# Position-bias features moved off GpSimd in an attention + soft-MoE kernel, with a new step order

## The chip, the core and the metric

One core of a Trainium2 chip runs the whole program. Its engines are PE (TensorE), DVE (VectorE), ACT (ScalarE), POOL (GpSimd) and SP (SyncE, which here only issues transfers). The metric is the device time of one execution in microseconds, as the median of three runs.

## What is computed

Attention with a position bias that a small network makes from relative positions, and behind it a soft mixture of experts over all 4608 tokens. All data are float32.

```python
# q, k, v: (8, 8, 576, 64); w1: (1, 32), b1: (32,), w2: (32, 8)
scores = q @ k.T / 8
x = log1p(|i - j|) / log1p(max(i, 1))              # one number per pair of positions
bias = relu(x[..., None] @ w1 + b1) @ w2           # 32 features, then 8 heads
attn = softmax(scores + bias) @ v                  # -> x: (4608, 512)
# phi: (512, 32); 8 experts, 4 slots each; w1: (8, 512, 1024), w2: (8, 1024, 512)
logits = x @ phi
slots  = softmax(logits, over tokens).T @ x        # 32 slots
slot_out[e] = relu(slots[e] @ w1[e]) @ w2[e]
out = softmax(logits, over slots) @ slot_out
```

## The kernel before

The program is a list of small steps. A string `ORDER` names every step once, and the steps' instructions are emitted in that order; each engine then runs its own instructions in the order in which they were emitted, and waits only for data and for buffers. A token such as `S1/5+@0,2` is step `S1` of unit 5, with the PSUM banks 0 and 2, and the `+` switches the step to its other form (another engine, or for `S` another way to cut the product). So `ORDER` alone decides queues, banks, and which engine takes a copy.

**Bias stage.** The bias depends on the position only through a table, so 36 jobs (`bias_job`) build it. A job i has four feature steps `f{i}.0` to `f{i}.3` (lines 925 to 934): each takes the table `tabs`, 304 to 576 wide by the job, times a scale, and clips it below. DVE and POOL do this with one `tensor_scalar` (line 933); ACT with a Relu (line 931). `B{i}` multiplies the four with the second layer (PE, line 944), `E{i}` copies the product out of PSUM with its constant (ACT line 957, DVE line 955), and `D{i}` writes it to DRAM (line 966). `b{c}` reads back the bias of a row stripe c of 128 query rows (line 390), once its eight jobs are written.

**Attention.** 40 units are (head pair, batch) pieces: 16 short ones for the first head pair, then 24 whole ones. In a unit `S{p}` makes the scores of 128 query rows for two heads, in 4 products of 128 rows (line 495) or, with `+`, in 8 of 64 rows (line 501); each product is two instructions. `t` adds the bias and finds the minimum (DVE, line 513), `e` is the exponential (ACT, line 521), `a` and `m` finish its sum (lines 528 and 532), `n` scales by it (POOL, line 398). `T` and `R` turn the result by 64-row pieces (`half_turn`, line 460), `c` and `cR` copy it out (ACT or DVE, line 401), `M0` to `M2` multiply with v (line 601), `x` copies, `xs` stores. `lq` and `lv` load q, k and v.

**Experts.** The units 32 to 39 also carry the tokens through the expert stage: `fx` fetches the stored heads (line 626), `K01`, `K23` and `KR` turn them, `L` makes logits (line 681), `lc` copies them, `D` sums them over heads, `d1` finds minima, `d2` is the exponential, `dq` keeps a copy of the logits, `W` and `C` turn, `Z` makes slot inputs. In units 38 and 39 `J` and `F` steps merge the two halves of the softmax. Then, all under unit 39: `F0` to `F7` are the experts' first layer (line 1029), `H` its Relu, `U0` and `U1` turn the hidden activations (line 1051), `V` copies them, `s{cg}.{Q}` is the second layer (line 1102), `so`, `g`, `ss` gather its result, `k` stacks the token weights, `o{cg}.{q}` and `X{cg}` make outputs (lines 1128 and 1142), `p` and `px` copy these out of PSUM, `P` (512 KB) and `PX` (256 KB) store them. `w`, `A` and `r` load the experts' 64 weight tiles of 512 KB (line 911). All of these transfers are issued by SP, in the order of `ORDER`.

## Time and profile before

| | |
|---|---|
| median of three runs | 574.61 us (574.53 to 574.68) |
| profiled execution | 575.72 us, of which span 573.9 us |
| busy in the span | PE 537.8, DVE 438.8, ACT 427.8, POOL 280.8 us |
| mean granted TensorE clock | 0.988 of full speed |

The span runs from the first to the last instruction. Each engine's busy time is the union of its instructions' times, so instructions that overlap count once. PE is busy in 94% of the span, and the idle part lies mostly in the first 80 us and behind 500 us. A "wait" line names who ended an engine's idle time; "issue" means that nothing in the profile explains the wait.

### The profile page before, as it was taken

What the parts mean: (1) busy time and instruction counts of PE and PEld (TensorE: products, weight loads), DVE (VectorE), ACT (ScalarE), POOL (GpSimd) and SP (SyncE); (2) the same over time, 40 slices, a digit from 0 to 9 for tenths busy, and PEclk for the clock granted to TensorE, in tenths of its full rate; (3) what the DMA queues carried; (4) which work ended last, traced back from release to release, by engine and by line L of the source; (5) the groups of instructions that cost most, each with busy time, mean ns of one, the idle gap of its engine ahead of it and who ended that gap; (6) DMA issues with size and microseconds to landing.
All of it is one profiled execution on the core that took longest, in us unless ns stands there. A gap on an engine that the chain in (4) does not pass through costs nothing.

```text
span 573.9 us, 23164 instructions
## 1 busy us (share of the span) xinstructions
PE 537.8 (94%) x9735; PEld 353.6 (62%) x9735; DVE 438.8 (76%) x1196; ACT 427.8 (75%) x935; POOL 280.8 (49%) x396
## 2 busy tenths in 40 slices
...
GB/s 136 269 198 208 204 175 326 286 295 278 250 118 138 136 55 126 183 245 89 158 189 167 81 100 211 162 270 154 269 98 122 105 61 284 326 334 366 334 333 327
DMA packets 46264, 117.12 MB, mean 204 GB/s; under 512 B 5457, under 2 KB 9681, under 8 KB 46161
## 3 DMA queue, kind: packets, MB, share of 16 engines
...
q10 hardware_dynamic: 144, 0.29, 0.2%
...
## 4 chain that ended last, share of the span: by engine, by line
PE 67%; DVE 11%; DMA 11%; ACT 4%; issue 3%; POOL 1%; DVEq 0%; SPq 0%; ACTq 0%
PE ps L601 19%; PE ps L460 15%; PE ps L501 14%; PE ps L495 5%; DVE mem L933 4%; DMA mem<-in_qk_dram 4%; DVE mem L513 4%; PE ps L944 3%; PE ps L1102 3%; PE ps L1029 2%; ACT mem L521 2%; DMA bias_m<-mem 2%; PE ps L681 2%; DMA xs<-mem 2%; DMA mem<-bias_m 1%
## 5 line engine op out<-in xcount | busy, mean ns | idle before, releaser
L398 POOL TENSOR_SCALAR mem<-mem,ms 128x576 f32<-128x576 f32 x288 | 212.4, 754 | 125.5 <-DVE ms L532 72.1
L513 DVE CUSTOM_DVE_ANT_0 mem<-ps,mem 128x576 f32<-128x576 f32 x288 | 207.9, 751 | 46.2 <-PE ps L501 31.9
L521 ACT ACTIVATE mem<-mem,ms 128x576 f32<-128x576 f32 x288 | 221.6, 774 | 24.8 <-DVE ms L513 21.4
L401 ACT COPY mem<-ps 128x1024 f32<-128x1024 f32 (+6 forms) x213 | 143.7, 698 | 53.9 <-PE ps L460 36.4
L601 PE MATMUL ps<-mem 64*64 64x288 f32 (+2 forms) x2880 | 161.8, 360 | 0.4
L401 DVE COPY mem<-ps 128x1024 f32<-128x1024 f32 (+6 forms) x143 | 114.4, 820 | 41.7 <-PE ps L1128 14.0
L501 PE MATMUL ps<-mem 64*64 64x64 f32 (+1 forms) x1648 | 125.0, 409 | 3.5 <-DVE ms L513 1.9
L460 PE MATMUL ps<-ident,mem 64*128 64x64 f32 x2976 | 119.8, 227 | 6.2 <-DMA mem<-xs 2.3
L460 PEld LDWEIGHTS ps<-ident,mem 64*128 64x128 f32 x2976 | 106.3, 140 | 25.8 <-issue 9.6
L601 PEld LDWEIGHTS ps<-mem 64*64 64x64 f32 x2880 | 98.8, 135 | 29.6 <-DVE ms L513 0.6
L501 PEld LDWEIGHTS ps<-mem 64*64 64x64 f32 x1648 | 68.1, 133 | 67.4 <-issue 46.5
L521 ACT ACTIVATION_READ_ACCUMULATOR mem<-mem,ms 128x1 f32 x288 | 55.9, 194 | 0.0
L495 PE MATMUL ps<-mem 64*128 64x512 f32 (+1 forms) x328 | 54.0, 435 | 1.5 <-DMA mem<-in_qk_dram 1.5
L933 POOL TENSOR_SCALAR mem<-mem,nb 128x336 f32<-128x336 f32 (+16 forms) x25 | 50.0, 2007 | 7.3 <-PE ps L944 4.0
L933 DVE TENSOR_SCALAR mem<-mem,nb 128x304 f32<-128x304 f32 (+17 forms) x81 | 49.2, 662 | 0.0
L528 POOL TENSOR_SCALAR ms<-ms 128x2 f32<-128x2 f32 x62 | 13.8, 223 | 71.3 <-ACT mem L521 68.4
L944 PE MATMUL ps<-mem,wbd 128*32 128x512 f32 (+41 forms) x480 | 38.4, 441 | 8.9 <-DVE mem L933 6.8
L495 PEld LDWEIGHTS ps<-mem 64*128 64x128 f32 x328 | 33.5, 187 | 20.0 <-issue 15.6
L944 PEld LDWEIGHTS ps<-mem,wbd 128*32 128x32 f32 x480 | 14.3, 109 | 28.0 <-issue 11.2
L957 ACT ACTIVATE mem<-ps,bcon 128x591 f32<-128x591 f32 (+20 forms) x35 | 19.7, 610 | 13.4 <-PE ps L944 13.3
L931 ACT ACTIVATE mem<-mem,cols 128x560 f32<-128x560 f32 (+15 forms) x38 | 27.2, 764 | 1.9 <-DVE mem L1204 1.7
L532 DVE RECIPROCAL ms<-ms 128x2 f32<-128x2 f32 x144 | 21.9, 160 | 6.7 <-POOL ms L528 5.1
...
## 6 DMA issues: line engine op xcount, KB each, us to landing
...
mem<-in_qk_dram SPq DMA_DIRECT2D x32, 576.0 KB, 4.6
...
mem<-bias_m SPq DMA_DIRECT2D x20, 576.0 KB, 5.4
...
```

The lines of the kernel that those rows point to most:

```text
L398: nc.gpsimd.tensor_scalar(out=out, in0=y, scalar1=r, scalar2=1.0, op0=ALU.mult, op1=ALU.mult)
L401: (nc.vector.tensor_copy if eng else nc.scalar.copy)(out=out, in_=in_)
L460: nc.tensor.matmul(out, src[rs], ident[rs, rs], is_transpose=True, start=True, stop=True, tile_position=(64 * r, 0))
L495: nc.tensor.matmul(pss[hh].t[:, n, 0:w], x[rs, S + QP[p]:S + QP[p] + P], x[rs, ks], start=True, stop=True, tile_position=(64 * hh, 0))
L501: nc.tensor.matmul(pss[hh].t[64 * r:64 * r + 64, n, 0:w], x[rs, q0:q0 + 64], x[rs, ks], start=True, stop=True, tile_position=(64 * hh, 64 ...
L513: nc.vector.tensor_tensor_reduce(out=d["y", p][:, :, hh], in0=blocks(d["ps", p][hh].read().rearrange("a n j -> a (n j)")[:, 0:S]), in1=blo ...
L521: nc.scalar.activation(out=y, in_=y, func=AF.Exp, bias=d["mn", p][:, hh:hh + 1], scale=-1.0, accum_out=d["sm", p][:, hh:hh + 1])
L532: nc.vector.reciprocal(out=r, in_=r)
L601: nc.tensor.matmul(d["po"].t[64 * c:64 * c + 64, hh, 0:n], d["v"][rs, 64 * k:64 * k + 64], turned(u)[rs, k, c, cs], start=k == 0, stop=k = ...
L931: nc.scalar.activation(out=f, in_=tabs[:, 0:n], func=AF.Relu, bias=cols[:, 1:2], scale=sc)
L933: (nc.gpsimd if eng else nc.vector).tensor_scalar(out=f, in0=tabs[:, 0:n], scalar1=sc, scalar2=nb1[:, 0:1], op0=ALU.mult, op1=ALU.max)
L944: nc.tensor.matmul(x[32 * t:32 * t + 32, o0 + c0:o0 + c1], wbd, f, start=True, stop=True, tile_position=(0, 32 * t))
```

## The change

Three edits in code, and a new `ORDER` for all 2649 steps.

- The features: a `+` on a feature step now always means ACT. Before, a `+` on the fourth feature of a job (`t = 3`) meant POOL. Of the 144 features DVE had 81, ACT 38 and POOL 25; now DVE has 94, ACT 50 and POOL none.
- `turn_hidden`: the 8 turns of 128x128 for each half become 16 turns of 64 rows, and `keep_hidden` reads the new layout. The copies keep their size.
- In the new order `dq` stands behind `d2` throughout ("logits' copy behind their exponentials").

```diff
         def feats(eng, t):
             f = fb[t] = room(FW * place_of["f"][f"f{i}.{t}"], n)
             sc = scl[:, scales[t]:scales[t] + 1]
-            relu[t] = eng and t < 3
-            if relu[t]:
+            relu[t] = eng
+            if eng:
                 nc.scalar.activation(out=f, in_=tabs[:, 0:n], func=AF.Relu, bias=cols[:, 1:2], scale=sc)
             else:
-                (nc.gpsimd if eng else nc.vector).tensor_scalar(out=f, in0=tabs[:, 0:n], scalar1=sc, scalar2=nb1[:, 0:1],
-                                                                op0=ALU.mult, op1=ALU.max)
+                nc.vector.tensor_scalar(out=f, in0=tabs[:, 0:n], scalar1=sc, scalar2=nb1[:, 0:1], op0=ALU.mult, op1=ALU.max)
...
     def turn_hidden(Q):
         h = ends["U", Q] = Banks(2, 2)
-        for z in range(2):
-            for x in range(4):
-                nc.tensor.transpose(out=h.t[:, z, x * P:(x + 1) * P], in_=ends["hS", Q][:, z, x * P:(x + 1) * P],
-                                    identity=ident)
+        for x in range(8):
+            for r in range(2):
+                half_turn(h.t[:, r, 64 * x:64 * x + 64], ends["hS", Q][:, x // 4, x % 4 * P:x % 4 * P + P], r)
...
-        cp(z, hT2[Q][:, 4 * z:4 * z + 4, :], ends["U", Q].read()[:, z].rearrange("a (x n) -> a x n", x=4))
+        cp(z, hT2[Q].rearrange("a x (r n) -> a r x n", r=2)[:, z], ends["U", Q].read()[:, z].rearrange("a (x n) -> a x n", x=8))
...
 ORDER = """
-f11.0/-1 f11.1/-1 f14.1/-1+ f14.2/-1+ f15.0/-1+ f11.2/-1 f14.3/-1 f11.3/-1+ f14.0/-1 wm/-1 f15.3/-1+ B11/-1@0
...
+f11.2/-1+ f13.1/-1 f13.3/-1+ f10.3/-1+ f13.2/-1 f13.0/-1 wm/-1 f10.2/-1+ f11.1/-1+ B13/-1@0 f11.0/-1+ f9.1/-1+ f9.0/-1+
...
```

The step marks also move in number: of the `S` steps 41 were cut in whole 128-row products and 30 are now; of the 36 `E` copies 25 were on ACT and 23 are now.

How the engines' queues change, at three places. First POOL at the start of the program. L933 is a feature, L528 the step `a`, L398 the step `n`, `nb_96` the clipping constant. Before:

```order
masks.py:199 AFFINE_SELECT ident<-ident 128x128
L933 TENSOR_SCALAR mem<-mem,nb_96 128x400
L933 TENSOR_SCALAR mem<-mem,nb_96 128x336
L933 TENSOR_SCALAR mem<-mem,nb_96 128x368
L933 TENSOR_SCALAR mem<-mem,nb_96 128x432
L933 TENSOR_SCALAR mem<-mem,nb_96 128x336
```

Now:

```order
masks.py:199 AFFINE_SELECT ident<-ident 128x128
L528 TENSOR_SCALAR ms<-ms 128x2 x2
L398 TENSOR_SCALAR mem<-mem,ms 128x9x64 x2
L528 TENSOR_SCALAR ms<-ms 128x2
L398 TENSOR_SCALAR mem<-mem,ms 128x9x64 x3
```

The features that opened POOL's queue are gone, and its first work is the scaling of the first exponentials.

Second PE at the last unit's expert stage, from the last product with v (L601) on. L460 is a 64-row turn (of `et`: `W`; of `lq`: `C`; of `mem`: `K01`, `K23`, `KR`), L862, L872 and L876 are `J` steps, L681 is `L`, L823 and L826 are `Z/38`, L696 and L698 are `D`, L882 is `F2` of the merge. Before:

```order
L601 MATMUL ps<-mem 64x288 x36
L862 MATMUL ps<-ident,stM_82 1x128 x2
L460 MATMUL ps<-ident,et_81 128x64 x3
L460 MATMUL ps<-ident,mem 128x64 x16
L460 MATMUL ps<-ident,lq 128x64 x3
L681 MATMUL ps<-mem,phis 32x288 x16
L872 MATMUL ps<-ident,et 128x1
L823 MATMUL ps<-mem,ek 32x512 x4
L826 MATMUL ps<-mem,ek 32x128 x4
L696 MATMUL ps<-lp,rsum 32x512
```

Now:

```order
L601 MATMUL ps<-mem 64x288 x36
L460 MATMUL ps<-ident,et_81 128x64 x3
L460 MATMUL ps<-ident,lq 128x64 x3
L862 MATMUL ps<-ident,stM_82 1x128 x2
L681 MATMUL ps<-mem,phis 32x288 x16
L872 MATMUL ps<-ident,et 128x1
L823 MATMUL ps<-mem,ek 32x512 x4
L826 MATMUL ps<-mem,ek 32x128 x4
L696 MATMUL ps<-lp,rsum 32x512
```

The turn `C` (of `lq`) moved ahead of the first step that reads the fetched heads, that first step is now `L` and no longer `K01`, and `K01` stands behind `D`.

Third SP at the end of the program: the weight loads, then the stores of 512 KB (L1136 before, L1134 now) and of 256 KB (L1151, now L1149). Before:

```order
L911 DMA mem<-in_moe_w_dram 128x1024 x28
L1136 DMA out_dram<-mem 128x1024 x8
L1151 DMA out_dram<-mem 128x512
L1136 DMA out_dram<-mem 128x1024 x4
L1151 DMA out_dram<-mem 128x512 x2
L1136 DMA out_dram<-mem 128x1024 x3
```

Now:

```order
L911 DMA mem<-in_moe_w_dram 128x1024 x28
L1134 DMA out_dram<-mem 128x1024 x3
L1149 DMA out_dram<-mem 128x512 x2
L1134 DMA out_dram<-mem 128x1024 x4
L1149 DMA out_dram<-mem 128x512
L1134 DMA out_dram<-mem 128x1024 x8
```

Three large stores now precede the first two small ones (`PX1`, `PX2`) where eight did. On PE the second layer's third column group (`s2`) and the small outputs `X0` to `X2` now stand directly behind `o0.0` and `o0.1`, ahead of `o1.0` and `o1.1`.

## Rows read from the trace of the kernel before

**Rows 1.** The page: busy time of each engine, its share of the span, and instructions.

```profile
PE 537.8 (94%) x9735; PEld 353.6 (62%) x9735; DVE 438.8 (76%) x1196; ACT 427.8 (75%) x935; POOL 280.8 (49%) x396
```

**Rows 2.** Busy time by stretch: PE, PEld, DVE, ACT, POOL, clock, DMA share, GB/s.

```profile
5.20:35.20 30.00, 22.65 (x302) 10.61 (x301) 29.86 (x55) 21.71 (x34) 29.68 (x16) 1.00 0.56 199
...
5.20:93.80 88.60, 76.80 (x1162) 43.66 (x1161) 85.50 (x196) 72.05 (x138) 70.25 (x59) 0.98 0.63 209
...
200.00:300.00 100.00, 99.20 (x1736) 67.08 (x1736) 80.39 (x224) 82.48 (x185) 54.29 (x85) 1.00 0.45 146
```

**Rows 3.** PE's waits between 5 and 94 us: total us, times, longest.

```profile
PE ps L944 <- DVE mem L933: 6.8, 7, 2.3
PE ps L944 <- DVE ms L513: 1.9, 3, 1.2
```

**Rows 4.** Features alone by stretch: DVE and POOL (L933), then ACT (L931).

```profile
5.20:93.80 88.60, 49.20 (x81) 49.23 (x25) 0.98 0.63 209
...
35.20:93.80 58.60, 20.18 (x32) 19.55 (x9) 0.97 0.66 214
...
5.20:93.80 88.60, 26.36 (x37) 0.98 0.63 209
```

**Rows 5.** Timeline of DVE and POOL: start, us, engine, line, count, idle before.

```profile
38.28 1.38 DVE L933 TENSOR_SCALAR mem<-mem,nb 128x496 f32<-128x496 f32 x3
...
38.98 6.95 POOL L933 TENSOR_SCALAR mem<-mem,nb 128x448 f32<-128x448 f32 x3 [4.02 <-PE ps L944]
...
49.01 4.50 POOL L398 TENSOR_SCALAR mem<-mem,ms 128x576 f32<-128x576 f32 x6
...
50.62 0.83 DVE L933 TENSOR_SCALAR mem<-mem,nb 128x448 f32<-128x448 f32 x1
```

**Rows 6.** The page's groups: score products by form, count, busy, mean ns, idle before.

```profile
L501 PE MATMUL ps<-mem 64*64 64x64 f32 (+1 forms) x1648 | 125.0, 409 | 3.5 <-DVE ms L513 1.9
...
L495 PE MATMUL ps<-mem 64*128 64x512 f32 (+1 forms) x328 | 54.0, 435 | 1.5 <-DMA mem<-in_qk_dram 1.5
```

**Rows 7.** Timeline of PE: the first two scores of unit 8, S0 and S3.

```profile
93.81 2.27 PE L501 MATMUL ps<-mem 64*64 64x512 f32 x32
```

**Rows 8.** Timeline of PE and ACT at the last expert stage; busy time by stretch.

```profile
505.38 1.12 PE L460 MATMUL ps<-ident,mem 64*128 64x64 f32 x16 [2.31 <-DMA mem<-xs]
...
506.26 0.42 PE L460 MATMUL ps<-ident,lq 64*128 64x64 f32 x3
...
512.51 0.63 ACT L401 COPY lp<-ps 64x576 f32<-64x576 f32 x1 [1.29 <-DVE mb L719]
...
505.38:517.83 12.45, 11.46 (x200) 6.88 (x200) 7.52 (x23) 5.28 (x12) 0.38 (x2) 0.86 0.79 293
```

**Rows 9.** Timeline of PE: turns by 64 rows, the hidden activations' turns, the second layer.

```profile
52.32 0.71 PE L460 MATMUL ps<-ident,mem 64*128 64x64 f32 x16 [0.33 <-DVE ms L513]
...
531.70 1.97 PE L1051 MATMUL ps<-ident,mem 128*128 128x128 f32 x16
...
542.45 0.41 PE L1102 MATMUL ps<-mem 128*32 128x128 f32 x4 [1.68 <-issue]
```

**Rows 10.** Timeline of the outputs: products, second layer, stores issued by SP.

```profile
544.32 2.06 PE L1128 MATMUL ps<-cT,ss 32*128 32x512 f32 x16
...
546.80 7.99 SPq L1136 DMA_DIRECT2D out_dram<-mem  x8
...
549.02 3.70 PE L1102 MATMUL ps<-mem 128*32 128x128 f32 x128
...
552.65 0.50 PE L1142 MATMUL ps<-small,ss 32*128 32x128 f32 x8
...
554.90 1.15 SPq L1151 DMA_DIRECT2D out_dram<-mem  x1
```

**Rows 11.** Busy time and DMA by stretch at the end, columns as in rows 2.

```profile
547.50:571.50 24.00, 15.35 (x338) 10.73 (x332) 8.67 (x12) 8.62 (x13) 0.00 (x0) 0.90 1.00 392
540.78:542.45 1.67, 0.00 (x0) 0.00 (x0) 0.00 (x0) 0.00 (x0) 0.00 (x0) 1.00 0.91 361
```

More of the change, by code (lines that the diff above doesn't have):

```diff
@@ new lines @@
+a3/34+ n2.1/34 t2.0/35#0 a4/34+ m4/34 m3/34 t2.1/35 n4.0/34 n3.1/34 W/32@0 KR/32@4 wc/32 T1/34@6 w20/39 w10/39 w21/39
+w22/39 w11/39 w8/39 w12/39 lq/36 lv/34 R1/34@0 x/33+ lv/35 fx/33 krc/32+ n3.0/34 T0/34@2 krd/32 c1/34 cR1/34+ T2/34@4
+c2/34 S3/35+@0,6 c0/34+ t3.0/35#1 t3.1/35 e2.0/35 S0/35@2,4 T3/34@0 Z/32@6 t0.1/35#2 t0.0/35 R3/34@2 n4.1/34 e2.1/35
+e3.0/35 c3/34 R4/34@0 cR3/34+ cR4/34 zc/32 L/33@4 e0.0/35 lc/33 C/32@0 T4/34@2 cA/32 K23/33@6 kc23/33 S1/35+@4,0
+c4/34+ t1.0/35#5 t1.1/35 S0/36+@2,6 e3.1/35 a3/35 e0.1/35 t0.1/36#4 t0.0/36 m3/35 e1.1/35 K01/33@4 KR/33@0 krc/33+
@@ new lines @@
+krd/33 D/33@6 e1.0/35 d1/33 n3.0/35 d2/33 a2/35 a0/35+ e0.0/36 m0/35 a1/35 m2/35 n2.1/35 n0.0/35 n3.1/35 n0.1/35
+dq/33+ n2.0/35 M0/34@2 M1/34 S1/36+@0,6 t1.1/36#3 t1.0/36 m1/35 n1.1/35 M2/34 x/34+ lq/37 fx/34 W/33@6 e0.1/36 kc01/33
+wc/33 R3/35@4 T3/35@0 cR3/35 T2/35@6 c2/35 n1.0/35 S2/36@2,4 c3/35+ d3/33 t2.1/36#1 a0/36+ e2.1/36 e1.1/36 R1/35@0
+Z/33@6 cR1/35+ t2.0/36 e2.0/36 zc/33 S4/36@0,4 t4.0/36#0 T1/35@2 K23/34@6 t4.1/36 e1.0/36 c1/35 kc23/34+ L/34@0
+KR/34@4 lc/34 krc/34 T0/35@2 C/33@0 a1/36+ m1/36 krd/34+ c0/35 K01/34@6 D/34@5 cA/33 S3/36+@0,2 d1/34 t3.0/36#5 m0/36
@@ new lines @@
+kc01/34 d2/34 dq/34+ e4.0/36 e4.1/36 M0/35@6 S2/37+@0,4 fx/35 lq/38 M1/35 M2/35 n0.0/36 n0.1/36 t3.1/36 a2/36+ a4/36
+m4/36 n4.0/36 n4.1/36 t2.1/37#2 m2/36 n2.1/36 e3.0/36 e3.1/36 W/34@2 R4/36@4 lv/36 lv/37 t2.0/37 n2.0/36 e2.0/37 wc/34
+cR4/36 x/35+ T4/36@0 a3/36+ c4/36+ m3/36 n1.0/36 n1.1/36 n3.1/36 n3.0/36 T2/36@2 c2/36 S0/37@6,4 T0/36@0 Z/34@2 c0/36
+t0.1/37#0 d3/34 t0.0/37 R3/36@0 zc/34 S3/37@6,4 e2.1/37 t3.1/37#1 R1/36@2 cR3/36 e0.1/37 cR1/36 K01/35@0 K23/35@2
+kc01/35 a2/37+ kc23/35 t3.0/37 T3/36@4 T1/36@6 c3/36 c1/36+ L/35@0 lc/35 KR/35@2 krc/35 e3.1/37 e0.0/37 S1/37@4,6
@@ new lines @@
+e2.0/38 t3.1/38 d1/36 M0/37@0 e3.1/38 cB/33 d2/36 dq/36 m1/38 cC/32 S4/38@6,4 M1/37 t4.0/38#0 S3/39+@2,6 t4.1/38
+e3.0/38 a3/38+ M2/37 cB/35 e4.0/38 d3/36 m3/38 a2/38 n1.1/38 n0.0/38 n0.1/38 n1.0/38 e4.1/38 t3.0/39#4 C/36@2 KR/36@4
+t3.1/39 m2/38 x/37 cA/36 krc/36+ W/36@6 K23/36@0 T1/38@2 krd/36 wc/36 kc23/36+ cB/36 a4/38 n2.1/38 n3.1/38 lv/38
+n2.0/38 S1/39@4,6 R1/38@0 n3.0/38 m4/38 n4.1/38 c1/38 Z/36@2 t1.1/39#3 t1.0/39 n4.0/38 e3.0/39 cB/34 cR1/38 R4/38@0
+R3/38@6 zc/36 T4/38@4 cR4/38 cR3/38 e3.1/39 c4/38+ T2/38@0 S0/39@2,6 c2/38 A6/39 A1/39 fx/37 A2/39 A9/39 e1.0/39
@@ new lines @@
+T0/38@4 a3/39 m3/39 c0/38 L/37@0 t0.1/39#2 t0.0/39 T3/38@6 K01/37@2 lc/37 S2/39@0,4 c3/38+ kc01/37 e0.1/39 e0.0/39
+e1.1/39 t2.1/39#5 t2.0/39 KR/37@6 K23/37@2 D/37@4 d1/37 d2/37 a1/39+ m1/39 n1.0/39 n3.1/39 a0/39+ m0/39 n1.1/39
+n0.0/39 n0.1/39 krd/37 kc23/37+ e2.1/39 cC/33 dq/37+ M0/38@0 M1/38 M2/38 W/37@2 e2.0/39 d3/37 krc/37+ wc/37 T1/39@4
+T0/39@6 a2/39 m2/39 n2.1/39 A3/39 lv/39 A10/39 fx/38 A8/39 x/38 cC/34 A7/39 A4/39 R1/39@2 cR1/39+ c1/39 c0/39 Z/37@0
+K01/38@2 n2.0/39 n3.0/39 R3/39@4 A11/39 A5/39 A12/39 cR3/39 zc/37 L/38@6 lc/38 T3/39@0 T2/39@4 kc01/38+ c2/39 c3/39+
```

324 lines of the change are left out of this document (150 added, 174 removed).

## The prediction, made before the changed kernel was run

> **What bounds the kernel now.** I read the page first: PE is busy in 94% of the span [rows 1], so most of the time is PE's own work, and only two things can move it: PE's idle time, and how much work the order gives it. Next I read the busy times by stretch. In the middle PE leaves 0.8 of 100 us idle [rows 2]; nothing is to be won there but cheaper instructions. Between 5.2 and 93.8 us it is busy for only 76.8 of 88.6 us, so 11.8 us go there. DVE is what bounds that stretch: it is busy for 85.5 of 88.6 us, and in the first 30 us for 29.86 of 30 [rows 2]. PE's waits confirm it: 6.8 us for features that DVE makes and 1.9 us for DVE's bias additions are its longest ones there [rows 3]. ACT has 16.5 us free in the same stretch (72.05 busy). I end the stretch where PE starts the scores of unit 8, since all features and all but none of the bias products are done then [rows 7].
>
> At the end another thing bounds. From 547.5 to 571.5 us the DMA engines are full (share 1.00, 392 GB/s) with the stores [rows 11]: 16 of 512 KB and 4 of 256 KB are 9.4 MB, which is 24 us at that rate. There PE's work counts only as far as it lets the first stores begin and keeps the queue fed.
>
> The sum below is made on the profiled execution: 575.72 us, 1.82 us of it outside the span, 1.11 us above the median of 574.61. I take the differences over to the median.
>
> **The front, 5.2 to 93.8 us.** Before, the 81 features on DVE take 49.20 us, 0.61 each, and POOL's 25 take 49.23 us, 1.97 each [rows 4]. Three wide ones that DVE ran one after the other, while POOL stood idle until 38.98 us for most of their time, took 1.38 us together, 0.46 each [rows 5]. The mean feature on DVE is a bit narrower (429 wide against 496), so I take 0.45. So 81 x (0.61 - 0.45) = 12.7 us of DVE's time is lengthening by POOL, if all of it is. It goes with POOL's features. DVE pays 13 more features, 13 x 0.45 = 5.9 us, and two bias copies E that ACT gives up, which I price as a feature on ACT, 26.36 / 37 = 0.71 [rows 4], so 1.4 us. Busy after: 85.5 - 12.7 + 5.9 + 1.4 = 80.1 us. ACT pays 12 more features at 0.71 and loses the two copies: 72.05 + 8.5 - 1.4 = 79.2 us. Neither POOL nor PE is near that (PE 76.8).
>
> So after the change two engines have 80 us of work where one had 85.5. How much they idle no row shows. DVE as the only bound idled 3.1 us; ACT, bound by DVE, 16.5. Two engines of equal load that feed each other idle more than one; I take 6 us, twice DVE's, since ACT's queue opens with 10 features in a row and has no product to wait for early. That ends the stretch at 86 instead of 88.6: **-2.6 us**. The bounds: 80.1 + 3.1 = 83.2, that is -5.4; and ACT idling as now, 79.2 + 16.5 = 95.7, that is +7.1. Behind the stretch PE has work without end, so the gain stays.
>
> The rows on POOL's slowing can be set beside the Trainium skill, SBUF, "Who interferes with whom": a DVE `tensor_scalar` in its two-port mode and a GpSimd instruction take a shared port pair in turn, each for its whole length, and the other stands still. The trace agrees that both are slow together (0.61 and 1.97 us); by this rule the scaling steps that stay on POOL would still slow DVE, which gives the first rival below.
>
> **Scores.** 41 steps with whole products take 54.0 us, 1.32 each, and the 103 cut ones 125.0 us, 1.21 each [rows 6]. Eleven steps change form: 11 x 0.1 = **-1.1 us**, on PE and so on the path. Bounds 0 (neighbours on PE overlap them) and -1.5.
>
> **The last expert stage.** PE stands 2.31 us until the heads of the last batch are fetched [rows 8]. The turn C (0.42 us) now stands ahead of that wait, so it costs nothing: -0.4. Then from 505.38 to the first layer at 517.83 us PE works 11.46 of 12.45 us [rows 8]. Now L comes first, so lc, D and d1 start earlier while K01, K23 and KR still fill PE; and dq's 0.63 us on ACT no longer stand before d2 [rows 8]. Against it, the copy of K01 now precedes d2 on ACT. Of the 1.0 us of idle I take 0.6 as filled. Together **-1.0 us**, bounds 0 and -1.5. The fetch itself could land earlier or later; with the same six loads ahead or behind it I leave it.
>
> **The hidden turns.** The 16 turns of both halves took 1.97 us; sixteen turns of 64 rows take 0.71 us [rows 9], and the change has two such sets, 1.42: **-0.6 us**. The copies V are as large as before; one half's now lie beside first-layer products. PE's unexplained wait of 1.68 us just before the outputs [rows 9] falls into a stretch in which the DMA engines are still loading weights at 361 GB/s [rows 11]; I leave it where it is.
>
> **The stores.** Count from the start of `o0.0`, T. Before, T is 544.32, the first store is issued 2.5 us later and the transfers flow 0.7 us behind it (546.80, 547.5) [rows 10, 11]. Now three large stores come first, then SP, which issues in order, stands before PX1. The three hold 1.57 MB, 4.0 us at 392 GB/s, so they are done at T + 7.2. PX1 needs `o0` (2.06 us), `s2` (3.70 us), X0, g2, X1 and a copy: before, from X0's start at 552.65 to the issue at 554.90 it takes 2.25 us [rows 10]. So PX1 is issued at T + 2.06 + 3.70 + 2.25 = T + 8.0 and flows at T + 8.7: the DMA engines stand for 1.5 us in a stretch that was full. Even P0.0.1, whose data are ready at about T + 2.5, waits behind PX1 and PX2. **+1.5 us**; bounds +0.5 (if s2 can start under the copies' shadow and PX1 comes sooner) and +2.6 (if the second small store and P0.0.1 leave gaps too).
>
> **The sum.** -2.6 - 1.1 - 1.0 - 0.6 + 1.5 = -3.8 us. The median goes from 574.61 to **570.8 us**; the changed kernel's profiled execution would be some 572. The other moves of the new order (loads of q, k and v, the bias loads, copies that change between ACT and DVE) have no term: where PE waits for them now is 1.5 us in all for the whole products' q and k [rows 6], and a new order can win or lose about that.
>
> **Rivals.**
> 1. *POOL's scaling slows DVE as the features did.* For: beside six of them (4.50 us from 49.01) a DVE feature of 448 took 0.83 us instead of some 0.46 [rows 5], and DVE's 32 features after 35.2 us took 0.63 each, when most of POOL's work was scaling [rows 4]. Against: POOL's features filled 49 us there, the scaling steps take 0.75 each. If 32 features keep their 0.18 us of lengthening, DVE has 80.1 + 5.8 = 85.9 us and the front gives nothing: -1.2 us in all, 573.4. The change would then not do in the front what it says.
> 2. *The end is held by the weights, not by PE.* If PE's 1.68 us wait is one for the DMA engines to come free, what PE gains before it (1.0 + 0.6) is lost in it: -2.2, 572.4. With rival 1 too: 574.9.
> 3. *Slower: ACT becomes the bound of the front.* ACT now makes 50 features beside all exponentials, and each exponential that it makes late holds the scaling, the turns and the products behind it. It decides from the point where ACT idles more than 9.4 us between 5.2 and 93.8 (79.2 + 9.4 = 88.6); now it idles 16.5. At 16.5 the front costs +7.1 and the kernel takes 574.61 + 7.1 - 1.2 = 580.5; half way, at 13, some 577. For: until the first exponential ACT has 34 features and its bias copies, about 33 us of work against 22 in the first 30 us now. Against: DVE, no longer lengthened, delivers earlier.
>
> **How the numbers follow.** The forecast as summed, 567.5 to 573: 0.51. Rival 2 alone, about 572.4: 0.13. Rival 1, with or without rival 2, 573.4 to 574.9: 0.19. Rival 3, above 575.8: 0.17. A measurement of this kernel can tell about 0.2%, 1.15 us, from no change. So faster 0.64, the same 0.19, slower 0.17. The range leaves out the upper part of rival 3 and the front's best case with all else (-5.4 - 1.5 - 1.5 - 0.6 + 0.5 = -8.5): 567.3 to 576.0.
>
> **What would show it.** In the changed profile: DVE's features at 0.45 to 0.5 us each and the scores of unit 8 at about 91 us (front right); at 93.8 with features at 0.6 beside scaling (rival 1); ACT busy for nearly all of 5 to 90 us with DVE waiting for nothing else, and unit 8 at 96 or later (rival 3). L501's and L495's busy times should fall by 1.1 us together, PE's turns of the hidden activations to 1.4 us. The DMA rate should show a hole between the third store and PX1, some 7 to 9 us after the first output product; without one that term is wrong. If PE's 1.68 us wait grows to 3, it is rival 2. A new wait of PE in the middle, over 2 us in sum, would make the whole sum wrong, as no term covers it.

## The result, and the profile after

The changed kernel takes **559.7 us** (four runs, 557.52 to 562.1) where the kernel before takes 574.57 us beside it: a ratio of 0.974, with a 95% interval of 0.970 to 0.979. The prediction was 570.8 us with a range from 567.3 to 576.0. The direction was right; the gain is four times the forecast, and the time lies below the range. Ratios, here and below, leave out the few runs over 1.5% above the fastest of their kernel, and medians count all, so a ratio is not always the quotient of the medians beside it. The profiled execution took 558.18 us, 556.4 of it in the span, against 573.9 before. The spans differ by 17.5 us where the medians differ by 14.9, since this execution is 1.5 us below the median of its kernel and the one before was 1.2 above; the stages below share out the 17.5.

The page gives the first reading: busy time of each engine, as [rows 1].

```profile
PE 530.2 (95%) x9839; PEld 350.5 (63%) x9839; DVE 426.0 (77%) x1191; ACT 435.4 (78%) x943; POOL 234.7 (42%) x393
```

Of the 17.5 us by which the span fell, PE's busy time gives 7.6 (537.8 to 530.2) and its idle time 9.9 (36.1 to 26.2). To see where, I cut both spans at the same four events: the first score product of unit 8, the issue of the last batch's `fx`, the start of the first layer F0, and the issue of the first output store. Each row is one stage: its length, then busy time of PE, PEld, DVE, ACT and POOL, granted clock, DMA share, GB/s. Before:

```profile
0.00:93.85 93.85, 80.69 (x1182) 47.54 (x1182) 86.82 (x204) 74.39 (x141) 71.73 (x65) 0.98 0.63 207
93.85:497.46 403.61, 396.92 (x7502) 269.97 (x7501) 322.53 (x915) 329.86 (x748) 208.72 (x330) 1.00 0.53 178
497.46:517.83 20.37, 17.06 (x293) 10.13 (x292) 11.25 (x39) 7.72 (x20) 0.38 (x2) 0.92 0.86 311
517.83:546.80 28.97, 27.11 (x440) 14.85 (x436) 8.81 (x28) 6.58 (x15) 0.00 (x0) 1.00 0.87 345
546.80:573.90 27.10, 16.05 (x340) 11.09 (x338) 9.37 (x12) 9.24 (x14) 0.00 (x0) 0.87 0.89 349
```

After:

```profile
0.00:83.05 83.05, 77.42 (x1227) 44.83 (x1227) 78.92 (x210) 78.52 (x154) 21.57 (x41) 1.00 0.74 248
83.05:480.98 397.93, 393.30 (x7537) 269.99 (x7533) 317.38 (x908) 334.19 (x744) 212.74 (x351) 1.00 0.54 179
480.98:498.24 17.26, 15.54 (x295) 9.54 (x293) 11.35 (x37) 6.91 (x18) 0.38 (x2) 1.00 0.94 351
498.24:527.67 29.43, 28.17 (x487) 15.44 (x484) 9.88 (x29) 6.32 (x14) 0.00 (x0) 1.00 0.84 333
527.67:556.40 28.73, 15.80 (x316) 10.73 (x308) 8.47 (x10) 9.50 (x16) 0.00 (x0) 0.85 0.84 330
```

The first two numbers of each row are the ones to compare. The front is 10.8 us shorter, and 7.5 of that is PE's idle time (13.16 to 5.63). The long middle is 5.7 us shorter, though no term of the prediction lay there. The last expert stage is 3.1 us shorter. From F0 to the first store it takes 0.5 us more, and from the first store to the end 1.6 us more.

**The front**, in the columns of [rows 2]:

```profile
5.20:35.20 30.00, 26.56 (x366) 12.93 (x365) 29.78 (x74) 29.28 (x50) 0.00 (x0) 1.00 0.66 229
5.20:83.01 77.81, 73.53 (x1210) 40.94 (x1210) 77.45 (x202) 76.06 (x151) 20.83 (x35) 1.00 0.75 253
```

The stretch ends, as before, where PE starts the scores of unit 8, now at 83.01 us. DVE is idle for 0.36 us of 77.81 and ACT for 1.75. PE's waits there answer [rows 3]; 6.8 us became 1.8:

```profile
PE ps L943 <- DVE mem L933: 1.8, 4, 1.0
PE ps L943 <- DVE ms L513: 1.5, 2, 1.2
```

The features alone by stretch, DVE's and then ACT's, answer [rows 4]. One on DVE takes 0.44 us (41.42 / 94), one on ACT 0.68:

```profile
5.20:83.01 77.81, 41.42 (x94) 1.00 0.75 253
...
5.20:83.01 77.81, 33.36 (x49) 1.00 0.75 253
```

**The clock.** Its mean over the front rose from 0.98 to 1.00, and over the last expert stage from 0.92 to 1.00. In the kernel before two stretches of the same columns show why; the line behind them is PE's at the first (start, us, count, idle before):

```profile
70.00:76.00 6.00, 5.65 (x94) 4.70 (x98) 4.57 (x14) 6.00 (x13) 3.68 (x5) 0.72 0.44 142
...
504.00:509.00 5.00, 3.62 (x53) 2.09 (x53) 1.92 (x8) 0.12 (x1) 0.38 (x2) 0.66 1.00 391
...
70.35 1.32 PE L501 MATMUL ps<-mem 64*64 64x512 f32 x10 [1.70 <-DVE ms L513]
```

A granted clock of 0.72 over 6 us and of 0.66 over 5 us means that PE ran at 1.2 instead of 2.4 GHz for part of each; I estimate from these rows that it lost 6 x 0.28 = 1.7 and 5 x 0.34 = 1.7 us. Before each, PE had stood still: 1.70 us for a bias addition of DVE, and the 2.31 us of [rows 8]. After the change no stretch between 5 and 535 us is below 1.00. The runs say the same: of the 83 in which the kernel before was timed beside the experiments, the 30 with a mean clock of 0.985 or less took 573.2 to 581.2 us, the 16 at 0.991 or more 569.1 to 576.0; all 16 runs of the changed kernel lie at 0.990 to 0.994.

**The stores** as SP issues them (start, us, count), and busy time and DMA share behind the third one, answering [rows 10, 11]:

```profile
527.67 1.64 SPq L1134 DMA_DIRECT2D out_dram<-mem  x3
532.51 1.68 SPq L1149 DMA_DIRECT2D out_dram<-mem  x2
534.24 3.23 SPq L1134 DMA_DIRECT2D out_dram<-mem  x4
...
532.00:534.00 2.00, 1.97 (x24) 1.16 (x20) 0.75 (x2) 1.42 (x4) 0.00 (x0) 1.00 0.56 205
534.00:536.00 2.00, 1.95 (x18) 0.90 (x12) 2.00 (x2) 1.69 (x3) 0.00 (x0) 1.00 0.71 272
536.00:538.00 2.00, 2.00 (x42) 1.15 (x40) 1.26 (x2) 2.00 (x3) 0.00 (x0) 1.00 1.03 408
```

The hole is there: 2 x 0.44 + 2 x 0.29 = 1.5 us of full transfer are missing. It lies on both sides of PX1, which SP issues at 532.51 us: behind the third large store, and again until the four large ones behind PX2 flow. There is a second loss, ahead of the first store. From T, the start of `o0.0`, that store took 2.5 us before (544.32 to 546.80, [rows 10]) and takes 4.1 now, with the first product slower and an unexplained wait in its weight loads:

```profile
523.60 2.94 PE L1126 MATMUL ps<-cT,ss 32*128 32x512 f32 x16
...
524.55 1.15 PEld L1126 LDWEIGHTS ps<-cT,ss 32*128 32x128 f32 x11 [0.66 <-issue]
```

From T to the end it is 29.6 us before and 32.8 now.

### The profile page after: what moved, and what is told of

It is laid out like the page before. It is cut to its first block, busy times and chain, and to the rows that moved or that the text cites. A ratio compares the mean times of both kernels' runs of the same rounds, so it can differ in the third digit from the quotient of the medians.

```text
span 556.4 us, 23360 instructions
## 1 busy us (share of the span) xinstructions
PE 530.2 (95%) x9839; PEld 350.5 (63%) x9839; DVE 426.0 (77%) x1191; ACT 435.4 (78%) x943; POOL 234.7 (42%) x393
## 3 DMA queue, kind: packets, MB, share of 16 engines
q8 instruction: 77, 1.26, 0.9%
## 4 chain that ended last, share of the span: by engine, by line
PE 73%; DVE 5%; DMA 4%; POOL 3%; issue 2%; ACT 2%; DVEq 0%; SPq 0%; POOLq 0%; ACTq 0%
PE ps L601 22%; PE ps L501 18%; PE ps L460 16%; PE ps L495 5%; PE ps L1100 3%; PE ps L1028 3%; POOL mem L398 3%; DVE mem L513 2%; PE ps L681 2%; DMA mem<-in_qk_dram 1%; PE ps L1126 1%; DMA mem<-bias_m 1%; DMA mem<-xs 1%; DVE mem L401 1%; PE ps L823 1%
## 5 line engine op out<-in xcount | busy, mean ns | idle before, releaser
L398 POOL TENSOR_SCALAR mem<-mem,ms 128x576 f32<-128x576 f32 x288 | 211.4, 749 | 125.4 <-DVE ms L532 82.6
L401 ACT COPY mem<-ps 128x1024 f32<-128x1024 f32 (+5 forms) x206 | 146.9, 735 | 56.4 <-PE ps L460 37.2
L601 PE MATMUL ps<-mem 64*64 64x288 f32 (+2 forms) x2880 | 160.7, 357 | 1.4 <-issue 0.6
L401 DVE COPY mem<-ps 128x1024 f32<-128x1024 f32 (+6 forms) x150 | 111.0, 757 | 37.7 <-PE ps L460 18.9
L501 PE MATMUL ps<-mem 64*64 64x64 f32 (+1 forms) x1824 | 137.7, 409 | 0.3 <-DMA mem<-in_qk_dram 0.2
L460 PE MATMUL ps<-ident,mem 64*128 64x64 f32 x3008 | 120.2, 227 | 4.1 <-POOL mem L398 1.4
L460 PEld LDWEIGHTS ps<-ident,mem 64*128 64x128 f32 x3008 | 107.5, 140 | 23.8 <-issue 10.4
L501 PEld LDWEIGHTS ps<-mem 64*64 64x64 f32 x1824 | 76.4, 133 | 69.5 <-issue 50.7
L601 PEld LDWEIGHTS ps<-mem 64*64 64x64 f32 x2880 | 97.7, 133 | 29.3 <-issue 1.4
L528 POOL TENSOR_SCALAR ms<-ms 128x2 f32<-128x2 f32 x84 | 18.6, 221 | 108.8 <-ACT mem L521 104.0
L933 DVE TENSOR_SCALAR mem<-mem,nb 128x368 f32<-128x368 f32 (+17 forms) x94 | 41.8, 516 | 0.1
L943 PE MATMUL ps<-mem,wbd 128*32 128x512 f32 (+40 forms) x480 | 38.0, 440 | 3.8 <-DVE mem L933 1.8
L495 PE MATMUL ps<-mem 64*128 64x64 f32 (+1 forms) x240 | 38.7, 435 | 0.1
L931 ACT ACTIVATE mem<-mem,cols 128x400 f32<-128x400 f32 (+17 forms) x50 | 34.3, 740 | 1.6 <-DVE mem L1202 1.6
L495 PEld LDWEIGHTS ps<-mem 64*128 64x128 f32 x240 | 24.1, 188 | 12.5 <-issue 10.2
L513 DVE DVE_READ_ACCUMULATOR2_ANT ms<- 128x1 f32 x288 | 24.1, 84 | 0.0
L956 ACT ACTIVATE mem<-ps,bcon 128x591 f32<-128x591 f32 (+24 forms) x35 | 18.5, 583 | 0.9 <-PE ps L943 0.7
## 6 DMA issues: line engine op xcount, KB each, us to landing
mem<-in_qk_dram SPq DMA_DIRECT2D x32, 576.0 KB, 4.4
mem<-bias_m SPq DMA_DIRECT2D x20, 576.0 KB, 5.1
```

The source lines that it names most:

```text
L398: nc.gpsimd.tensor_scalar(out=out, in0=y, scalar1=r, scalar2=1.0, op0=ALU.mult, op1=ALU.mult)
L401: (nc.vector.tensor_copy if eng else nc.scalar.copy)(out=out, in_=in_)
L460: nc.tensor.matmul(out, src[rs], ident[rs, rs], is_transpose=True, start=True, stop=True, tile_position=(64 * r, 0))
L495: nc.tensor.matmul(pss[hh].t[:, n, 0:w], x[rs, S + QP[p]:S + QP[p] + P], x[rs, ks], start=True, stop=True, tile_position=(64 * hh, 0))
L501: nc.tensor.matmul(pss[hh].t[64 * r:64 * r + 64, n, 0:w], x[rs, q0:q0 + 64], x[rs, ks], start=True, stop=True, tile_position=(64 * hh, 64 ...
L513: nc.vector.tensor_tensor_reduce(out=d["y", p][:, :, hh], in0=blocks(d["ps", p][hh].read().rearrange("a n j -> a (n j)")[:, 0:S]), in1=blo ...
```

## The experiments

My theory after the result: the loads of the front were priced right, and what failed is the idle time that I allowed two engines of equal load. The rivals: the new order gains in the middle whatever the front does; or a price (features, score form, turns, stores) was wrong. Each set of runs was measured on one chip, the sets on different ones. The kernel before was measured again with each set and gave medians from 573.9 to 576.4 us; ratios are to its runs in the same set. Names with `o_` start from the order of before, names with `n_` from the new one, and `h_` are half of each.

### Who makes POOL's features

**o_new_code**: the old order with the new rule for `+`, so that all 25 POOL features go to ACT. It and o_split also have the new turns of the hidden activations.

```diff
-            relu[t] = eng and t < 3
-            if relu[t]:
+            relu[t] = eng
+            if eng:
```

> The old order with the new code: all 25 features that POOL made go to ACT, nothing else moves but the turns of the hidden activations (64-row pieces). Theory 1 (the front gained because DVE and ACT carry equal loads and no POOL feature lengthens DVE): ACT gets 25 x 0.68 = 17 us on top of the 72 us it has before unit 8, 89 us in all, so ACT takes DVE's place as the bound and little is won: 571 to 578 us. Rival (POOL's features alone held the front, whoever makes them instead): 562 to 567 us. If the order alone counts: 574 us.

**o_split**: the same, but every second of the 25 loses its mark, so that 13 go to DVE and 12 to ACT, nearly the deal of the new kernel in the old order.

```diff
-f11.3/-1+ ... f15.3/-1+ ...
+f11.3/-1 ... f15.3/-1+ ...
```

> The old order with the new code, and POOL's 25 features dealt out in turn, 13 to DVE and 12 to ACT, as the changed kernel has them in number; places in the order unchanged. Theory 1: loads before unit 8 fall to about 77 us on DVE and 80 on ACT against 85.5, so the scores of unit 8 start at 86 to 89 us instead of 93.8, and the time is 566 to 570 us; the new order's part of the front is what is missing to 83 us. Rival (the order alone made the gain): 574 us, the freed time turns into waits. Rival (POOL alone): 562 to 565 us.

**n_pool**: the new order, but the rule of before, so that its 12 marked fourth features run on POOL.

```diff
-            relu[t] = eng
+            relu[t] = eng and t < 3
```

> The new order, with the old rule for the fourth feature: its 12 features marked with + go from ACT back to POOL, at their places. Theory 1: each lengthens DVE by some 0.5 us and takes POOL 2 us, DVE loses 6 us before unit 8: 563 to 567 us. Rival (the order alone made the gain): 558 to 561 us as the changed kernel, or faster since ACT has 8 us less.

Measured: o_new_code 578.88 us (ratio 1.007, 1.002 to 1.012), o_split 569.35 us (0.990, 0.987 to 0.994), n_pool 563.41 us (0.981, 0.973 to 0.988). The front of each, up to the end of the last bias product (81.66 us in the changed kernel), in the same columns; first o_new_code, then o_split, then n_pool:

```profile
5.20:98.43 93.23, 78.63 (x1166) 43.33 (x1166) 74.09 (x196) 86.95 (x163) 20.55 (x34) 0.93 0.59 198
```

```profile
5.20:88.00 82.80, 76.44 (x1166) 43.57 (x1168) 79.66 (x209) 78.69 (x150) 21.10 (x34) 0.98 0.67 223
...
5.20:88.00 82.80, 43.60 (x94) 0.98 0.67 223
```

```profile
5.20:87.98 82.78, 75.43 (x1176) 42.06 (x1175) 79.42 (x198) 68.67 (x136) 45.46 (x45) 0.98 0.69 235
...
5.20:87.98 82.78, 44.49 (x94) 25.92 (x12) 0.98 0.69 235
```

The second row of o_split has DVE's features alone, that of n_pool DVE's and POOL's.

With none left on POOL and none given to DVE, ACT is the bound (86.95 of 93.23 us), and PE's longest wait is for it (first row; the second is from n_pool):

```profile
PE ps L940 <- ACT mem L928: 9.2, 3, 4.3
```

```profile
PE ps L941 <- POOL mem L930: 2.6, 1, 2.6
```

So rival 3's mechanism is real, and the even deal is what avoids it. The median of o_split lies in the range of its first theory (566 to 570 us), that of o_new_code 0.9 us above its own (571 to 578). o_split is the cleanest look at my front term: DVE 79.66 us of work and ACT 78.69, where I had worked out 80.1 and 79.2. But the stretch, which in the kernel before ends its bias products at 93.89 us, ends them at 88.00: DVE idles 3.1 us as it did before, not 6. In the new order it idles 0.4. Giving 12 features back to POOL costs 3.7 us in the medians (563.41 against 559.7) and 6.6 us in the profiled spans (563.0 against 556.4). The median is in the range of the first theory (563 to 567), but the two kernels were timed on different chips and the intervals of their ratios overlap (0.973 to 0.988, 0.970 to 0.979). Of the 6.6 us, 1.7 are a clock drop at 28 us, behind the wait of 2.6 us for POOL.

### Front, middle and end apart

**h_front_new**: the new order up to unit 8's first scores, the old one behind it, with the old hidden turns. **h_front_old**: the old front with POOL's features, the new order behind it. At the joint 18 and 36 steps had to take other buffers, and some other banks.

```diff
-... B32/-1@6 D30/-1 E32/-1 S0/8+@0,4 ...
+... E32/-1+ a1/5 n2.1/5 ... D32/-1 S0/8@6,4 ...
```

> The new order up to the first scores of unit 8, with the new features; all steps behind that in the old order, with the old turns of the hidden activations. At the joint, 18 buffers for scores change place and banks that are taken are replaced by free ones. Theory 1 (front 9 to 11 us of the 15, the rest from the middle and the expert stage): 563 to 566 us, scores of unit 8 at 83 us. Rival (the front gives some 5 us and the middle the rest): 568 to 571 us.

> The front (up to the first scores of unit 8) in the order of before, with POOL's 25 features; everything behind it in the new order, with the new turns. Theory 1 (the front carries its gain through the whole kernel, since the new order keeps PE fed behind it): PE has 12.5 to 13.5 us idle in the first 80 us as before, the last bias product starts at about 91.9 us instead of 80.5, and the whole 10 to 11 us stand in the time: 569 to 571 us, with the last batch's heads stored some 10 us later than the changed kernel (480.98). Theory 2 (most of the gain is made in the middle and at the end, and a slow front is partly caught up there): 563 to 566 us.

**n_end_old**: the new order up to `M2` of unit 39, then the old one, with the old hidden turns.

```diff
-M2/39 fx/39 W/38@6 C/37@1 J1/38@3 ... L/39@4 ...
+fx/39 M2/39 A13/39 J1/38@1 W/38@2 ... K01/39@6 x/39+ C/37@4 J2/38 L/39@2 ...
```

> The new order up to the last batch's M2, then the order of before for the last expert stage and the outputs, with the old hidden turns. From the issue of the last heads' store to the first layer's start F0 it took 20.37 us before and 17.26 after, from F0 to the outputs 26.49 and 25.36, from there to the end 29.6 and 32.8. Theory 1 (the order of the stage itself makes the difference): 20.4, 26.5 and 29.6 us here, so the sum of 75.4 becomes 76.5 and the time is about 561 us, 1 us more than the changed kernel; TensorE's granted clock falls to 0.50 again for two slices after the wait for the heads. Theory 2 (the wait and the clock drop before the last expert stage came from what the old middle left behind, not from this order): F0 comes after 17 to 18 us, the end takes 29.6 us, and the time is 557 to 558 us.

Measured: h_front_new 569.7 us (0.992, 0.988 to 0.995), h_front_old 571.59 us (0.9935, 0.990 to 0.997), n_end_old 556.57 us (0.968, 0.963 to 0.973). With the old front in place, the scores of unit 8 start at 95.10 us instead of 83.01, the last `fx` is issued at 495.56 us instead of 480.98, and the kernel takes 571.6 us, 0.6 above the range of its first theory and far from the second: nearly the whole gain is gone, so what the front saves is not caught up elsewhere. h_front_new fell to the rival (568 to 571 us), not to my theory. It keeps the short front (last bias product at 81.3 us, though unit 8 starts at 85.18) but issues its last `fx` at 493.41, only 4.05 us before the old kernel. Between 80 and 200 us PE idles 5.9 us there against 2.0 in the changed kernel:

```profile
80.00:200.00 120.00, 114.14 (x2314) 82.83 (x2312) 91.84 (x258) 94.59 (x221) 68.63 (x111) 0.99 0.61 201
```

It also has a clock drop of 1.7 us at 92 us. How much of this is the joint's doing isn't shown, and h_front_old waits at its joint too. So the two halves can't be added up exactly: by the profiles the front is worth between 9 us (7.5 of idle time and 1.7 of clock, by the stages) and 12 us (95.10 less 83.01), but by the medians h_front_new has only 5 us of the gain.

n_end_old fell to theory 2. With the old last expert stage behind the new front and middle, `fx` to F0 takes 16.5 us and the clock stays at 1.00; n_tail_old below, with the same outputs but the new last expert stage, has the same median (556.48). The same kernel measured twice (n_tail_old and n_tail_old2, below) took 17.6 and 20.2 us for it. In the second one PE stood for 1.01 us at 497.1, after 0.96 us at 465.9, and then had the second of these rows (n_tail_old's stands first):

```profile
497.00:505.00 8.00, 7.91 (x82) 2.97 (x84) 2.67 (x11) 0.94 (x3) 0.00 (x0) 1.00 1.02 392
```

```profile
497.00:505.00 8.00, 7.29 (x81) 4.41 (x84) 4.07 (x15) 1.96 (x5) 0.00 (x0) 0.57 1.02 386
```

0.43 of 8 us is 3.4 us lost, twice 1.7, in one execution of a kernel and not in the other. Of all profiles, the three with a clock drop in this stage took 20.2 to 20.8 us for it (the kernel before, and n_oldturn and n_tail_old2 with the new order of the stage), and the others 16.4 to 18.3 us with the new order and 16.5 to 18.9 with the old.

### The form of the scores

**o_quarters** and **n_quarters**: all whole score steps cut by 64 rows, 41 in the old order and 30 in the new.

```diff
-S0/8@6,4
+S0/8+@6,4
```

> The kernel before with all 41 whole score steps cut by 64 rows; nothing else. Theory 1 (a cut step takes 0.10 us less of PE, as the rows of before show, 1.32 against 1.21 us): the line of whole products is gone, the two forms together take 174.9 instead of 179.0 us, and about 4 us are saved where PE is the bound: 571 us. Theory 2 (2.6 us less for 11 steps, as the two traces show, is 0.24 a step): 9.7 us less, 565 us. Theory 3 (the scores' time only moves between neighbours that overlap on PE, and the 2.6 us of the two traces come from the clock): 574 to 575 us, no change.

> The changed kernel with its 30 whole score steps cut by 64 rows as well. In the kernel before, cutting all 41 took 4.4 us off PE's busy time in the scores (0.107 a step) and yet gave no time, since PE then waited more for DVE's bias additions. Theory 1 (there DVE was the bound of the front; here it is balanced, and PE's time counts in the middle): 3.2 us less of PE's busy time, and 1.5 to 3 us less in the time. Theory 2 (a cut step lets its two banks go later to DVE, and PE waits for it whatever the front does): PE's waits for DVE's bias additions grow by about as much, and the time is the same within 1 us or longer.

Measured: o_quarters 579.05 us (1.009, 1.004 to 1.013) and n_quarters 560.63 us (0.976, 0.972 to 0.980; the changed kernel beside it 559.38). The group of the scores in o_quarters, count, busy, mean ns, idle before:

```profile
L498 PE MATMUL ps<-mem 64*64 64x512 f32 (+1 forms) x2304 | 174.6, 414 | 5.5 <-DVE ms L510 4.2 <-DMA mem<-in_qk_dram 1.2
```

The busy time falls from 179.0 to 174.6 us, 0.107 a step as [rows 6] had it, and the kernel gets slower, by more than any of the three theories had it. Two things show. PE now waits longer for DVE's bias additions (4.2 us there, 1.9 in [rows 6]). And PE's time isn't less. I count each instruction from its start to the start of the next, less PE's idle time between them, from unit 8 to the last `fx`. So counted, scores of both forms take 139.7 us in the kernel before and 139.8 in o_quarters, 136.4 in the changed kernel and 137.4 in n_quarters; and turns take 101.7 and 105.0, 102.0 and 102.9. The profile of o_quarters has a clock drop of 1.7 us there, at 441 us. Without it, cutting all steps costs PE 1.7 us in scores and turns together, and 1.8 in the new order. The timeline of the kernel before shows what the line's busy time hides:

```profile
300.27 1.15 PE L501 MATMUL ps<-mem 64*64 64x512 f32 x16
301.24 1.64 PE L601 MATMUL ps<-mem 64*64 64x288 f32 x24
...
315.30 1.25 PE L495 MATMUL ps<-mem 64*128 64x512 f32 x8
316.48 1.33 PE L501 MATMUL ps<-mem 64*64 64x512 f32 x16
317.74 3.08 PE L460 MATMUL ps<-ident,mem 64*128 64x64 f32 x72
```

From start to start a cut step takes 0.97 us ahead of products (300.27 to 301.24) and 1.26 ahead of a turn (316.48 to 317.74); over all steps of the middle, there and in the changed kernel, it is 1.03 and 1.16 to 1.19, and a whole step ahead of a turn 1.12 to 1.14. So I asked whether the neighbour sets the price. **o_fit** makes 13 cut steps ahead of turns whole and cuts 2, **n_fit** makes 7 whole in the new order:

```diff
-S1/4+@2,4
+S1/4@2,4
```

> The kernel before with the form of 15 score steps chosen by what PE does next: 13 cut steps that stand before a turn become whole, 2 whole ones that stand before products become cut. 52 whole steps instead of 41. Theory 1 (the form has no price of its own; from one start to the next, a cut step takes 1.02 us before products and 1.17 before a turn, a whole one 1.12 before a turn, and a turn takes 0.13 us less before a whole step): PE's time for scores and turns falls by 13 x 0.05 to 13 x 0.18, that is 0.7 to 2.3 us, although more steps are whole; time 572 to 575 us. Theory 2 (the form has its price, 0.107 us a step, as the busy times of the two lines say): 11 more whole steps add 1.2 us; 575 to 576 us.

> The changed kernel with 7 cut score steps that stand before a turn made whole (37 whole steps instead of 30). Theory 1 (the neighbour sets the price): PE's time for scores and turns falls by 7 x 0.05 to 7 x 0.18, 0.4 to 1.3 us; the time is the changed kernel's or up to 1.3 us less. Theory 2 (the form sets it): 0.7 us more.

Measured: o_fit 577.32 us (1.003, 1.000 to 1.005), n_fit 559.66 us (0.974, 0.971 to 0.977). Scores and turns together, counted in the same way: 241.4 us before and 243.5 in o_fit, of which 1.7 are again a clock drop, at 442 us; 238.5 in the changed kernel and 238.3 in n_fit. The three profiles of the changed kernel give 238.0 to 238.6, so neither theory's gain or loss shows: the neighbour as the price is not confirmed, and o_fit took longer than both theories said (572 to 576). What is settled: the busy time of a line of short matmuls is no price. Cutting every step brought nothing in the new order and 0.9% more time in the old.

### The hidden turns and the stores

**n_oldturn**: the old 16 turns of 128 rows. **n_tail_old**: the outputs in the old order, eight large stores first. **n_tail**: one step moved, so that a fourth large store fills the hole. **n_fit_tail**: n_fit with the old outputs.

```diff
 # n_oldturn
-        for x in range(8):
-            for r in range(2):
-                half_turn(...)
+        for z in range(2):
+            for x in range(4):
+                nc.tensor.transpose(...)
 # n_tail_old
-... s2.0/39@4 s2.1/39 X0/39@0,2 ... P0.0.0/39 P0.1.1/39 ... P0.1.0/39 ... PX1/39 ... PX2/39 P0.0.1/39 ...
+... o1.0/39@4,6 ... s2.0/39@4 s2.1/39 ... P0.0.1/39 P0.0.0/39 P1.0.1/39 P1.1.0/39 ... P1.0.0/39 ... PX1/39 ...
 # n_tail
-P0.0.0/39 P0.1.1/39 ... PX1/39 ... PX2/39 P0.0.1/39 o1.0/39@6,2
+P0.0.0/39 P0.0.1/39 P0.1.1/39 ... PX1/39 ... PX2/39 o1.0/39@6,2
```

> The changed kernel with the hidden activations turned as before (16 turns of both halves after the whole first layer). Theory 1 (the two sets of 64 rows save 0.6 us, as predicted, or the 1.1 us by which the stretch from F0 to the outputs fell): that stretch is 26.0 to 26.5 us instead of 25.4, and the time 0.6 to 1.1 us longer. Theory 2 (the wait that stands before the outputs takes up what is saved): the stretch stays at 25.4 us and the time at that of the changed kernel.

> The changed kernel with the output products and stores in the order of before (eight large stores first), all else as changed. Theory 1 (the new order of the stores costs about 3 us, twice the 1.5 us of the prediction): the stretch from the first output product to the end falls from 32.8 to 29.6 us, and the time by about 3 us against the changed kernel beside it, to 556.5 us. Theory 2 (the end is the DMA engines' work, and a later tail only shows that PE came early): the stretch stays above 31 us and the time within 1 us of the changed kernel.

> The changed kernel itself, beside the three others, so that they are compared on one chip. Every theory: the time of its first measurement, 559.7 us (557.5 to 562.1), with the last heads stored at about 481 us, 17.3 us from there to the first layer F0, 25.4 from F0 to the outputs and 32.8 from there to the end.

> The changed kernel with one step moved: the fourth large output product and its store now stand before PX1's small store, so that four large stores are issued before SP waits for PX1. Theory 1 (the hole between the third store and PX1 costs time): the fourth store fills 1.3 us of it, and the time falls by 1 to 1.5 us against the changed kernel, to about 558.5 us, with the DMA engines' share from 520 to 540 us above the 0.64 of the changed kernel. Theory 2 (the end is set by PX2 and the eight stores behind it): the hole moves, and the time stays at 559.5 to 560 us.

> The changed kernel with the fourth large store moved ahead of PX1 once more, now beside the changed kernel on one chip. Theory 1 (filling the hole between the stores gains 1 to 1.5 us, and its first time of 557.06 us beside 559.4 to 559.7 for the changed kernel was that): 1 to 2.5 us less than the changed kernel here. Theory 2 (the stretch from the first output product to the end was only 0.4 us shorter, 32.4 against 32.8 us, and the rest was chance between chips): the two are within 0.5 us.

> The changed kernel itself, for that comparison. Every theory: 559.4 to 559.7 us, as in its two measurements so far.

> The same 7 steps made whole in the version with the old order of the outputs, the fastest so far (556.5 us). Theory 1: 555.2 to 556.5 us, and faster than both kernels. Theory 2: 557.2 us.

> The version with the old order of the outputs once more, beside the one with the 7 steps made whole. Every theory: 556.5 us again, with 30 to 31 us from the first output product to the end.

| | median, us | ratio (95%) | F0 to first store | first store to end |
|---|---|---|---|---|
| before | 574.57 | | 28.97 | 27.10 |
| after | 559.7 | 0.974 (0.970 to 0.979) | 29.43 | 28.73 |
| after_again | 559.38 | 0.974 (0.970 to 0.979) | 30.24 | 28.36 |
| after_third | 557.68 | 0.971 (0.965 to 0.977) | 29.52 | 28.45 |
| n_oldturn | 560.03 | 0.973 (0.968 to 0.979) | 29.87 | 28.97 |
| n_tail | 557.06 | 0.968 (0.964 to 0.972) | 30.17 | 27.81 |
| n_tail2 | 557.88 | 0.969 (0.964 to 0.974) | 29.75 | 27.79 |
| n_tail_old | 556.48 | 0.9695 (0.965 to 0.9735) | 29.06 | 27.10 |
| n_tail_old2 | 558.13 | 0.970 (0.966 to 0.975) | 28.86 | 27.19 |
| n_fit_tail | 558.38 | 0.972 (0.969 to 0.976) | 28.10 | 27.27 |
| n_end_old | 556.57 | 0.968 (0.963 to 0.973) | 28.90 | 27.17 |

In the last column the order alone decides: 27.1 to 27.3 us for eight stores first (also in the `o_` kernels and h_front_new), 27.8 with four, and 28.4 to 29.0 with three (28.1 in n_fit and 29.2 in h_front_old). So the hole costs 1 to 2 us in the profile. Counted from T to the end the difference is larger: 29.6 to 30.8 us with eight first, 32.5 to 33.0 in the three profiles of the changed kernel. Beside after_again, n_tail_old was 2.9 us faster, as its first theory had it. But n_tail_old2, for which I expected 556.5 us again, took 558.13, and n_fit_tail, with 558.38 beside it, missed both its theories. The single moved store took 0.6 to 0.9 us out of the last stage, but on one chip n_tail2 and the changed kernel came out the same (557.88 and 557.68): theory 2. The fastest medians are those of n_end_old and n_tail_old, some 0.5% below the changed kernel; their intervals overlap with its own, so that they beat it is likely and not shown.

n_oldturn can't be told from the changed kernel. From F0 to T it is 25.36 us after, 26.49 before, and 26.70 in n_oldturn, of which 0.9 are a clock drop that ends in this stretch. So the new turns save 0.4 us or so up to T. But the first store leaves no sooner (column four): it left 2.5 us after T before and leaves 4.1 to 4.6 after it in the three profiles of the changed kernel. Why is not shown.

## Why the prediction was right or wrong

**The front: the step that failed.** The prices held (DVE's features 0.45 forecast, 0.44 measured; ACT's 0.71 and 0.68; loads of 80.1 and 79.2 us against 79.66 and 78.69 in o_split; in the changed kernel itself 77.45 and 76.06, since the new order has less other work in the stretch). The sentence that failed is the one after them, "Two engines of equal load that feed each other idle more than one; I take 6 us". Rows gave 3.1 us for DVE, and I doubled it on an argument. o_split kept 3.1 and so reached my lower bound of -5.4; the new order came to 0.4 and passed it. The bound was none: "DVE idles as now" is what the old order leaves, and the change brought another. Front: forecast -2.6 us, measured -10.8 by the stages. Of the 8.2 us between them, 5.6 are this idle time and 2.6 the smaller load of DVE.

**What had no term.** The middle is the second step that failed. I read 0.8 us of idle time in one stretch of 100 us, took it for the whole middle and wrote that nothing was to be won there but cheaper instructions; it had 6.7 us of idle time, and 5.7 us were won. I also wrote that a new wait would make the sum wrong, and did not price old waits that go. The clock is the larger part of these: two drops of 1.7 us each, visible in my own rows as 0.98 and 0.86 [rows 2, 8], behind waits of PE. The first wait was one for DVE, which my front term relieved, so its 1.7 us could have stood in the sum as a chance. The second went too, but not by the change's order there, as n_end_old shows. PE's waits of 1.5 us for q and k of whole products [rows 6] fell to 0.1.

**Scores, -1.1.** The two lines fell by 2.6 us (179.0 to 176.4), and yet the term was wrong in kind: cutting 41 and 30 steps cost PE 1.7 and 1.8 us. I read overlap as price. That the sign came out right is luck.

**Last expert stage, -1.0.** It fell by 3.1 us, but 1.6 of that is waiting and 1.5 busy time at the low clock. With the old order it took as little (16.5 us, at best 16.4 with the new). The order of L, C and dq is worth nothing that shows; as one order gave 16.4 to 18.3 us without a clock drop, 1.0 us could hide there.

**Hidden turns, -0.6.** Right for the turns, 1.97 us before and twice this line now:

```profile
506.96 0.71 PE L460 MATMUL ps<-ident,mem 64*128 64x64 f32 x16
```

Up to T it is -1.1, with an unexplained wait that fell from 1.68 to 1.02 us, and at the first store nothing.

**Stores, +1.5.** Right for the hole: 1.5 us, +1.6 in the stage behind the first store, and 1 to 2 by the experiments. But I counted from T, and from T to the end it is +3.2, above my upper bound of +2.6: I let the first store leave 2.5 us after T, as before, and it left 4.1 after it.

**The rivals.** Rival 1 (POOL's scaling) fell: DVE's features took 0.46 us in o_split, beside all the scaling and with no feature on POOL. Rival 2 (weights hold the end) fell by its own sign: the wait before the outputs was 1.0 us, not 3. What it priced came in another place: the 1.1 us gained up to T were gone at the first store. Rival 3 did not happen, since ACT idled 1.75 us and not 9.4; o_new_code shows that it would have with an uneven deal.

**The middle, 5.7 us, stays open in part.** PE idles 2.1 us less there, and by the count from start to start its scores take 3.3 us less (139.7 to 136.4); turns and products with v differ by 0.4 or less. The new order of the middle makes this, not the front: in the eleven profiles with that order and its forms the scores take 136.0 to 137.0 us, with either front and either end, and in the kernel before, o_new_code and o_split 139.6 to 139.7. More of them stand ahead of products (85 steps of 128 against 71), where a step is shorter. That this neighbourhood is the cause was argued and not confirmed: o_fit and n_fit did not show it.

**What a measurement can tell.** I took 0.2%. The changed kernel's 16 runs spread from 556.4 to 562.1 us and the 83 later ones of the kernel before from 569.1 to 581.2, so differences of 1 or 2 us between single kernels are not decided here.
